# Attention and gated MLP in one kernel: the plain part in three chunks of 512 tokens in place of four of 384

## The chip, the cores and the metric

The kernel runs on one core of a Trainium2 chip. The metric is the device time of one execution in microseconds (us); 943.36 us is the median of three runs before the change (943.19 to 943.65). TensorE (PE in the profile; PEld is its weight load), VectorE (DVE), ScalarE (ACT), GpSimd (POOL) and SyncE (SP) each work through a queue of their own in order and wait on semaphores for one another. SP, ACT and POOL also issue the DMA transfers.

## The reference

Eight sequences of 576 positions, 8 heads of 64: attention with a causal window of 32 positions (heads 0 to 3) or of 32 positions four apart (heads 4 to 7), and then a gated MLP over all 4608 tokens, in float32:

```python
scores = scale * np.matmul(q, k.transpose(0, 1, 3, 2))      # (8, 8, 576, 576)
mask_plain = (rel >= 0) & (rel < window)                    # window = 32
mask_dil = (rel >= 0) & (rel < window * dilation) & (rel % dilation == 0)   # dilation = 4
attn = exp(scores - max) / (sum + 1e-9)                     # masked
x = np.matmul(attn, v)  ->  (4608, 512)
g = x @ w_gate                                              # 512 x 1536
y = (g * (1.0 / (1.0 + np.exp(-g))) * (x @ w_val)) @ w_out  # 1536 x 512
```

## The kernel before

**Precision.** Every MLP product is made of three matmuls in the type fp32r: a float32 operand is split into a high part (a cast) and a low part (operand minus high part), and high x high, high x low and low x high are added in PSUM.

**Two parts of the MLP.** The first T0 = 1536 tokens are the *plain part*: NPLAIN = 4 chunks of CH = 384 tokens. The other 3072 tokens go through a Strassen scheme (seven products in place of eight) in NCS = 3 chunks of two times 512 tokens, whose matmuls are those of L773.

**A step of the plain part** is one of the NF = 12 blocks of 128 hidden units of one chunk; there are NS = NPLAIN x 12 = 48 steps, `s` in the main loop. In a step, `gv_mm` (L459) makes 12 matmuls for the gate into `bank_g` and 12 for the value into `bank_v`, `act_tanh` (ACT, L468), `dve_u` (L473) and `dve_h` (L478) form h, `h_hi` (ACT, L483) and `h_lo` (POOL, L488) split it, and `out_mm` (L496) of the step before adds 12 matmuls to four output banks. So a step has 36 matmuls. `out_store` empties the output banks once in a chunk.

**Attention** is cut into *packs*: a pair of heads, a stretch of tokens, up to four *groups* of four blocks of 32 queries against 64 keys. The list of packs has 46 packs with 152 groups in all. A pack's work: `scores` (PE, L354, two heads x four blocks x groups matmuls of 64 columns; for the first packs the mask is added by two more, L348), `shift` (DVE, maximum L368 and subtraction L369), `exps` (ACT, L374), `turn_e` (PE, one transpose per group, L378), `keys` (ACT copy, L384), `results` (PE, L394), `norm` (DVE, L403 to L405), `turn_y` (PE, one transpose per group, L412), and a copy into the x of the MLP: high part by ACT (L429, or L444 in the head) and low part by DVE (L430, L448), or for Strassen chunks a plain copy (L438). Packs from the fifth on are placed by hand into *slots*, three to a step, in a table `visit`: at slot "A" of pack m the results of pack m-1 and the scores of m, at "B" the transposes.

**The head.** The four packs of chunk 0 (three groups each) run first, together with the first weight units, in an order for PE, DVE and ACT that is written out as a string: Q scores, S shift, X exps, T turn_e, K keys, A results, N norm, U turn_y, H and L the two parts of x, W0 to W4 the five stages of the next weight unit. What follows in the program is put in order by the framework's list scheduler, which may also set matmuls of the first step between those of the string; on the chip each engine then keeps that order.

**Weights.** The float64 weights come as 24 units of 768 KB (`w_load` on SP). Two units make the weights of one of the 12 hidden blocks; unit 2f has the gate and half of the value columns, unit 2f+1 the rest. Five stages turn them into high and low parts: E (ACT, L235), T (L253 on ACT or L256 on DVE, by `by_act`), B (DVE, L263 or L266), H (ACT cast, L274), L (POOL, L278). All 24 are made during the steps of chunk 0, by `w_upto`, two a step. Raw units lie in six buffers.

**Mixing.** During the later chunks the weights are combined for the Strassen part and written to DRAM in pieces: 9 x NP = 54 stages (`mix_stage`, DVE L650 to L663, ACT L660), called from the main loop by `mix_to` twice a step from step 12 on, `half * 54 // 62` of them by half step `half`, so the last at half step 62.

Of the kernel before, what the change touches and what calls it, by code (L numbers as in the profile page):

```python
# [11 lines left out]
F32R = mybir.dt.float32r  # L12
# [6 lines left out]
P = 128  # L19
D = 64  # L20
S = 576
DIL = 4
CH = 384
DM = 512
# [18 lines left out]

NPLAIN = 4
CS = 512
# [15 lines left out]
T0 = NPLAIN * CH  # L61
KINDS = "aoooFooboooo"
NM = len(KINDS)

# [71 lines left out]
def attention_moe(ctx, tc, qkb, vb, w, masks, ident, out):  # L136
# [3 lines left out]
    def pk(m):  # L140
        return PACKS[m]
# [5 lines left out]
    M_ATT = M_SMALL + 40  # L147
    M_X1 = M_ATT + QKB + 4 * NGM * (D + 1) + 3 * TP
    M_SPARE = M_X1 + 2 * NK * CH
    NSPARE = 1352  # L150
    M_H = M_SPARE + NSPARE
    M_RAW = M_H + 5 * CH
    M_X0 = M_RAW + 8 * WU
    M_W = M_X0 + 2 * NK * CH
    M_RING = M_W + NT * 4 * CS
    M_HQ = M_RING + NAT * PIECE
    assert M_HQ + 5 * NP * CS <= M_W + 2 * WB * NF
    M_LOW = M_RAW + PIECE
    M_OT = M_LOW + 2 * PIECE + CS
    assert M_OT + 4 * CH + 2 * CS <= M_X0  # L160
    origin = -(-nc.sbuf_base // 64) * 64
# [24 lines left out]
    consts = at(0, (NM * BK + P) // 2, BF16)  # L186
    mask_sb, ident16 = consts[:, :NM * BK], consts[:, NM * BK:]

# [5 lines left out]

    WARM = 24
    wt = [at(M_W + 2 * WU * u, 2 * WU, F32R) for u in range(NU)]

# [12 lines left out]
    loaded = 0  # L210
    raw_at = [M_RAW + 2 * WU * n for n in range(4)] + [M_LATE + 2 * WU * n for n in range(2)]
    raw_of = {}
    YW = 3 * UT + 8

    def w_load():
        nonlocal loaded
        u = loaded
        n = u % 6 if u < NU - NLAST else (u + 2) % 4
# [20 lines left out]
    def by_act(u):  # L239
        return u in (1, 2) or u > 3 and u % 2 == 1  # L240

# [3 lines left out]
    def w_shift(u):  # L245
        n = u - NU + NLAST
        y = at(M_LATE + 4 * WU + YW * (u % 3) if n < 0 else M_SPARE if n == 0 else raw_at[(u + 1) % 4], YW, I32)
        wst[u]["y"] = y[:, :3 * (UT + 1)].rearrange("p (a b) -> p a b", a=3)[:, :, :UT]
# [65 lines left out]
    early, later = {}, {}  # L314
    for k, n, fn, fb in (("qk", QKB, FQ, 4), ("v", 4 * NGM * (D + 1), 4 * FG * (D + 1), 3), ("e", TP, P * FG, 2),
                         ("y", TP, P * FG, 2), ("pt", TP, P * FG, 2)):
        later[k] = Ring(n, o)
        o += n
    o = M_ATT
    for k, fn, fb in (("qk", FQ, 4), ("v", 4 * FG * (D + 1), 3), ("e", P * FG, 2), ("y", P * FG, 2), ("pt", P * FG, 2)):  # L320
        step = -(-fn // 8) * 8
        early[k] = Ring(fn, *range(o, o + step * fb, step))
        o += step * fb
    assert o <= M_H
    for k, a in (("bm", M_SMALL), ("bz", M_SMALL + 16)):
# [84 lines left out]
    def turn_y(m, bank):  # L410
        for g in range(pk(m).ng):
# [3 lines left out]
    x32 = [[at(o, 2 * CS).rearrange("p (k c) -> p k c", k=2) for o in x]  # L415
           for x in ((M_OT + 4 * CH, M_X0), (M_SPARE, M_X0 + 2 * CS))]

    def x_views(m, bank, *x):
        if pk(m).ng * P == CH:
            return bank[:, :CH], *x  # L420
        n = len(pk(m).runs)
        return (bank[:, :P * pk(m).ng].rearrange("p (n t) -> p n t", n=n)[:, :, :CH // n],
                *(t.rearrange("p (n t) -> p n t", n=n) for t in x))

    def x_copies(m, bank):
        c = pk(m).chunk
        if c < NPLAIN:
            src, xh, xl = x_views(m, bank, *(t[c % 2][pk(m).pair] for t in (x_hi, x_lo)))
            nc.scalar.copy(out=xh, in_=src)  # L429
            nc.vector.tensor_tensor(out=xl, in0=src, in1=xh, op=ALU.subtract)  # L430
        else:
# [10 lines left out]
    def x_copy_hi(m, bank):  # L442
        src, xh, xl = x_views(m, bank, *(t[0][pk(m).pair] for t in (x_hi, x_lo)))
        nc.scalar.copy(out=xh, in_=src)  # L444

    def x_copy_lo(m, bank):
        src, xh, xl = x_views(m, bank, *(t[0][pk(m).pair] for t in (x_hi, x_lo)))
        nc.vector.tensor_tensor(out=xl, in0=src, in1=xh, op=ALU.subtract)  # L448
        st[m].clear()


# [11 lines left out]
    t_ring = Ring(CH, M_H, M_H + CH)  # L463
    hh_ring = Ring(CH, M_H + 2 * CH, M_H + 3 * CH)

# [20 lines left out]
    def h_lo(i):  # L486
        hl = at(M_H + 4 * CH, CH, F32R)
        nc.gpsimd.tensor_tensor(out=hl, in0=hst[i][0], in1=hst[i][1], op=ALU.subtract)  # L488
        hst[i][2] = hl
# [9 lines left out]
    def out_store(ci):  # L499
        for j in range(4):  # L500
            ot = at(M_OT + CH * j, CH)
            if j % 2 == 0:
# [13 lines left out]

    bank_x, bank_k, bank_r, *s_banks = [bank(ab, *x) for x in (("fx", 1), ("fk", 1), ("fr", 2), ("fs0", 2), ("fs1", 2))]


    load_qk(0, fa, nc.sync)  # L520
    nc.scalar.dma_start(out=consts, in_=masks)
    load_qk(1, fa, nc.scalar)
    load_v(0, fa, nc.sync)
    nc.sync.dma_start(out=idents, in_=ident.rearrange("n p c -> p n c"))
    nc.vector.memset(ones, 1.0)
# [4 lines left out]
    warm = ones.bitcast(BF16)  # L530
    for _ in range(WARM):
        nc.tensor.matmul(out=bank_x[:, :P], lhsT=warm, rhs=warm, start=True, stop=True)
    load_qk(2, fa, nc.sync)
    load_v(1, fa, nc.sync)
    w_load()
    load_qk(3, fa, nc.sync)
    load_v(2, fa, nc.sync)
    w_load()

    def more_in():  # L540
        load_v(3, fa, nc.sync)
        w_load()
        ready["w"] = True

# [6 lines left out]
        "U": lambda m: turn_y(m, x_bank[m]), "H": lambda m: x_copy_hi(m, x_bank[m]),  # L551
        "L": lambda m: x_copy_lo(m, x_bank[m]), "M": lambda m: more_in(), "W": lambda n: w_one(STAGES[n]),
# [26 lines left out]

    M1 = 4 * NPLAIN + 10  # L580
    for n in range(5):
        visits(4 + n, 5 + 13 * n // 2, 8 + 13 * n // 2)
    for n in range(4):
        visits(9 + n, 39 + 25 * n // 3, 43 + 25 * n // 3)
    for m in range(13, M1 + 1):
        a = SB - 75 + 49 * (m - 13) // 10
        visits(m, a, a + 3)
# [5 lines left out]
    def attend(now):  # L593
        what, m = visit.get(now, ("", 0))
        if what == "A":
# [6 lines left out]
            if m < NPK:  # L602
                shift(m, two, later, m < 8)
                exps(m)
                load_v(m, later, nc.scalar)
                if m + 1 < NPK:
# [23 lines left out]

    q_at = at(M_RAW, PIECE)
    l_at = at(M_LOW, 2 * PIECE, F32R).rearrange("p (n l c) -> p n l c", n=4, l=2)

# [80 lines left out]

    x1 = at(M_X0 + 4 * CS, 2 * CS).rearrange("p (k c) -> p k c", k=2)
    HS = 10
    own = [M_SPARE + 2 * CS, M_SPARE + 4 * CS, M_OT, M_X1 + 4 * CS]
    NOWN = len(own)
    assert own[1] + 2 * CS <= M_RAW
    kept = [[at(M_X1 + CS * (2 * k + r), CS) for r in range(2)] for k in range(2)]  # L720
    temps = [M_RAW + CS * n for n in range(7)] + [M_OT + 2 * CS]
    g_ring = Ring(CS, *temps[:3])
# [192 lines left out]
def layout(q, k, v, moe_w_gate, moe_w_val, moe_w_out):  # L915
# [17 lines left out]
    w = np.ascontiguousarray(w.reshape(NF, P, 2, WU).transpose(0, 2, 1, 3))  # L933
    masks = np.concatenate([block_masks(), np.eye(P)], axis=1).astype(ml_dtypes.bfloat16)
    order = np.arange(P).reshape(DIL, BQ).T.ravel()
# [21 lines left out]
```

## Time and profile before

| what | value |
| --- | --- |
| median of three runs | 943.36 us |
| the profiled execution: its time | 943.46 us |
| the profiled execution: its span | 941.7 us |
| PE, PEld, DVE, ACT, POOL busy | 99%, 86%, 67%, 42%, 26% of the span |
| first matmul of the plain part, its last run (L496) | starts at 19.8 us, holds the chain from 382.0 to 384.1 us |
| last run of matmuls | holds the chain from 921.4 to 938.0 us |

A profile's page lists the busy time of each engine, the span in 40 slices, the DMA queues, the chain of work that ended last, and the costliest groups of instructions. The chain in order of time gives for each piece its start and the time that it held the chain, in us; for a run of matmuls (x12) that is the time until the next piece takes over. In the timeline the two first numbers are start and length in us, and the brackets give the engine's idle time before the instruction and what ended it. A row of the groups ends in busy time in us and mean length of one in ns, then the idle time before them. A row of the stretches gives for each engine busy us and instructions, then the granted clock of TensorE, the share of the DMA engines and GB/s.

### The profile page before, as it was taken

The page shows a single profiled execution, that of the slowest core. Times are in us where ns is not written, and L with a number is a line of the kernel's source. Part 1 is how long each engine was busy: PE and PEld are TensorE (multiplying, and loading weights), DVE is VectorE, ACT ScalarE, POOL GpSimd, SP SyncE. Part 2 cuts the span into 40 slices and gives each one's busy share as a digit, 9 for nine tenths or more (in the row PEclk, how much of TensorE's full clock was granted, in tenths as well). Part 3 has the DMA queues.
Part 4 walks back from the last instruction along what each step waited for, and adds up shares of the span by engine and source line. Part 5 has one row for each costly group of instructions (what it writes and reads, how often), then busy time and mean ns, then how long its engine had stood idle before and what let it go on. Part 6 is the DMA issues. An engine that isn't in the chain of part 4 may idle for free.

```text
span 941.7 us, 21975 instructions
## 1 busy us (share of the span) xinstructions
PE 929.6 (99%) x9204; PEld 813.0 (86%) x9204; DVE 632.9 (67%) x1072; ACT 393.1 (42%) x687; POOL 249.4 (26%) x301
## 2 busy tenths in 40 slices
PE   7899999999999999999999999999999999999998
PEld 5799999999999999888888888888888888888886
DVE  4767566666677865666669965666689735656863
ACT  4885323233233333333344643343355523334451
POOL 0765421111111131123233121222223213343310
PEclk9999999999999999999999999999999999999999
DMA  9976156577757791676767768676766675656662
GB/s 370 337 283 200 36 203 214 177 238 238 242 183 243 248 323 43 219 237 213 236 215 236 245 219 260 222 240 199 255 202 197 210 257 186 198 186 195 198 207 107
DMA packets 75394, 205.26 MB, mean 218 GB/s; under 512 B 7584, under 2 KB 24096, under 8 KB 75296
## 3 DMA queue, kind: packets, MB, share of 16 engines
q0 software_dynamic: 27216, 99.10, 33.6%
q1 hardware_dynamic: 35696, 64.93, 19.4%
q10 hardware_dynamic: 12384, 39.83, 12.5%
q8 instruction: 72, 1.18, 0.5%
q14 instruction: 26, 0.21, 0.1%
HBM read 161.37 MB, written 42.47 MB: 216 GB/s over the span
## 4 chain that ended last, share of the span: by engine, by line
PE 96%; ACT 1%; DVE 1%; issue 1%; DMA 0%; DVEq 0%; ACTq 0%
PE bo L773 32%; PE bv L773 12%; PE bg L773 12%; PE bo L496 10%; PE bv L459 10%; PE bg L459 10%; PE two L394 3%; PE two L354 3%; PE two L378 2%; PE two L412 2%; DMA at_bfloat<-masks 0%; ACT at_float32r L274 0%; ACT at_int L235 0%; DVE at_int L266 0%; DVE at_int L263 0%
## 5 line engine op out<-in xcount | busy, mean ns | idle before, releaser
L773 PE MATMUL bo<-at_float32r 128*128 128x512 f32 x1296 | 308.5, 392 | 0.0
L773 PEld LDWEIGHTS bo<-at_float32r 128*128 128x128 f32 x1296 | 242.2, 188 | 51.9 <-ACT at_float L503 0.2
L701 POOL DMA_DIRECT2D at_float32r<-pieces x189 | 101.4, 537 | 381.0 <-PE bo L773 219.2
L736 DVE TENSOR_TENSOR at_float<-bo,at_float 128x512 f32<-128x512 f32 (+1 forms) x169 | 114.2, 684 | 106.0 <-ACT at_float L778 50.2
L736 DVE TENSOR_TENSOR at_float32r<-at_float,at_float32r 128x512 fp32r<-128x512 f32 (+1 forms) x147 | 115.1, 806 | 41.7 <-ACT at_float32r L763 28.7
L773 PE MATMUL bv<-at_float32r 128*128 128x512 f32 x486 | 130.0, 394 | 0.0
L773 PE MATMUL bg<-at_float32r 128*128 128x512 f32 x486 | 129.8, 393 | 0.0
L488 POOL TENSOR_TENSOR at_float32r<-at_float,at_float32r 128x384 fp32r<-128x384 f32 x48 | 54.8, 1142 | 220.2 <-PE bo L496 175.7
L459 PE MATMUL bg<-at_float32r,at_float32r 128*128 128x384 f32 x576 | 110.9, 339 | 2.1 <-DVE at_float L473 1.3
L459 PE MATMUL bv<-at_float32r,at_float32r 128*128 128x384 f32 x576 | 110.1, 338 | 0.0
L496 PE MATMUL bo<-at_float32r,at_float32r 128*128 128x384 f32 x576 | 110.1, 338 | 0.0
L773 PEld LDWEIGHTS bv<-at_float32r 128*128 128x128 f32 x486 | 90.2, 188 | 19.5
L773 PEld LDWEIGHTS bg<-at_float32r 128*128 128x128 f32 x486 | 90.3, 188 | 19.2
L763 ACT CAST at_float32r<-at_float 128x512 fp32r<-128x512 f32 x126 | 77.3, 622 | 69.7 <-PE bo L773 23.8
L459 PEld LDWEIGHTS bg<-at_float32r,at_float32r 128*128 128x128 f32 x576 | 99.9, 188 | 3.8 <-POOL at_float32r L278 1.1
L496 PEld LDWEIGHTS bo<-at_float32r,at_float32r 128*128 128x128 f32 x576 | 100.2, 188 | 0.9
L459 PEld LDWEIGHTS bv<-at_float32r,at_float32r 128*128 128x128 f32 x576 | 99.7, 188 | 0.8
L799 ACT ACTIVATE at_float<-at_float 128x512 f32<-128x512 f32 x72 | 45.6, 633 | 81.0 <-DVE at_float L736 80.8
L473 DVE SCALAR_TENSOR_TENSOR at_float<-at_float,bg 128x384 f32<-128x384 f32 x48 | 26.6, 554 | 76.8 <-ACT at_float L468 76.8
L778 ACT COPY at_float<-bg 128x512 f32<-128x512 f32 x63 | 37.0, 587 | 95.5 <-PE bg L773 95.3
L801 DVE SCALAR_TENSOR_TENSOR at_float<-at_float,at_float 128x512 f32<-128x512 f32 x72 | 49.5, 687 | 10.6 <-ACT at_float L799 10.5
L278 POOL TENSOR_TENSOR at_float32r<-at_int,at_float32r 128x768 fp32r<-128x768 f32 x24 | 45.8, 1917 | 40.7 <-ACT at_float32r L274 40.5
(79 smaller groups left out, 904.5 us busy)
## 6 DMA issues: line engine op xcount, KB each, us to landing
at_float32r<-pieces POOLq DMA_DIRECT2D x189, 512.0 KB, 3.9
pieces<-at_float32r SPq DMA_DIRECT2D x126, 256.0 KB, 4.6
at_int<-w SPq DMA_DIRECT2D x24, 768.0 KB, 6.2
at_float<-vb ACTq DMA_DIRECT2D x28, 390.0 KB, 5.0
at_float<-vb ACTq DMA_DIRECT2D x14, 520.0 KB, 5.2
at_float<-qkb ACTq DMA_DIRECT2D x14, 448.0 KB, 5.4
out<-at_float SPq DMA_DIRECT2D x23, 256.0 KB, 4.0
at_float<-qkb ACTq DMA_DIRECT2D x10, 544.0 KB, 6.0
```

What stands on the lines that cost most here:

```text
L278: nc.gpsimd.tensor_tensor(out=lo, in0=wst.pop(u).bitcast(F32), in1=hi, op=ALU.subtract)
L354: nc.tensor.matmul(out=two[BQ * j:BQ * j + BQ, h, a + BK * g:a + BK * g + BK], lhsT=t[r, q:q + BQ], rhs=t[r, k:k + BK], start=not masked, ...
L459: nc.tensor.matmul(out=bank[:, :CH], lhsT=wcol(f, o, low), rhs=x[ORDER[j]], start=n == 0, stop=n == len(ops) - 1)
L488: nc.gpsimd.tensor_tensor(out=hl, in0=hst[i][0], in1=hst[i][1], op=ALU.subtract)
L496: nc.tensor.matmul(out=bank_o[j][:, :CH], lhsT=wcol(f, 2 * DM + P * j, low), rhs=x, start=f == 0 and low == 0 and x is hh, stop=f == NF - ...
L701: nc.gpsimd.dma_start(out=taken[asked], in_=pieces[asked % NPIECE])
L736: engine.tensor_tensor(out=out, in0=a, in1=b, op=op)
L763: nc.scalar.copy(out=o[:, 0], in_=src)
L773: nc.tensor.matmul(out=bank, lhsT=w, rhs=x, start=first and n == 0 and t in FRESH, stop=last and n == len(ops) - 1, skip_group_check=True)
L778: nc.scalar.copy(out=kept[KEPT[t]][r], in_=banks[0][r][:, :CS])
L799: nc.scalar.activation(out=f, in_=g, func=AF.Tanh, scale=0.5)
L801: nc.vector.scalar_tensor_tensor(out=f, in0=f, scalar=1.0, in1=g, op0=ALU.add, op1=ALU.mult)
```

## The change

`CH` becomes 512 and `NPLAIN` 3, so the plain part has 36 steps of matmuls with 512 columns. The packs of the plain part are cut anew: four packs of 512 tokens (four groups each) for chunk 0, six for each of the chunks 1 and 2; the list again has 46 packs and 152 groups, and from the 17th on it is the same. The table `visit` follows: packs 4 to 10 every 13/3 slots in chunk 0, packs 11 to 26 every four slots from slot 37 on. Mixing is called at `half * 54 // 41`, so it ends at half step 41 after chunk 0 (step 32 of 36).

SBUF is shared out anew: the buffers of the four early packs move into the place of weight units 8 to 15, the transposed keys (`pt`) share the buffer of the scores (`e`), raw weights have five buffers in place of six, high parts of h one in place of two, and the Strassen part's buffers move. `h_hi` is written behind `out_mm` of the step before, which reads the one buffer.

The head: another string, other loads first (masks in two parts, the second late), 9 warm-up matmuls of 512 columns in place of 24 of 128, four more of them between the first packs (`Y2` twice), and other units whose stage T is done by ACT.

```diff
-CH = 384
+CH = 512
-NPLAIN = 4
+NPLAIN = 3
...
-    out = [Pack(c, p, CH * c, CH * c + CH) for c in range(NPLAIN) for p in ORDER]
+    out = [Pack(0, p, 0, CH) for p in ORDER]
+    for c, cut in ((1, 704), (2, 1280)):
+        a, b = CH * c, CH * c + CH
+        out += [Pack(c, p, lo, hi) for p, lo, hi in ((0, a, b), (2, a, cut), (1, a, b), (2, cut, b), (3, a, cut),
+                                                      (3, cut, b))]
...
-    WARM = 24
+    WARM = 9
...
-    raw_at = [M_RAW + 2 * WU * n for n in range(4)] + [M_LATE + 2 * WU * n for n in range(2)]
+    raw_at = [M_RAW + 2 * WU * n for n in range(3)] + [M_LATE + 2 * WU * n for n in range(2)]
...
-        return u in (1, 2) or u > 3 and u % 2 == 1
+        return u == 0 or u % 2 == 1
...
+    o = M_W + 16 * WU
+    for k, n, many in (("qk", FQ, 4), ("v", 4 * FG * (D + 1), 4), ("e", P * FG, 4), ("y", P * FG, 2)):
...
+    for x in early, later:
+        x["pt"] = Ring(x["e"].n, *x["e"].starts)
...
-    hh_ring = Ring(CH, M_H + 2 * CH, M_H + 3 * CH)
+    hh_ring = Ring(CH, M_H + 2 * CH)
...
-    for _ in range(WARM):
-        nc.tensor.matmul(out=bank_x[:, :P], lhsT=warm, rhs=warm, start=True, stop=True)
+    def idle(n):
+        for _ in range(n):
+            nc.tensor.matmul(out=bank_x.rearrange("p (a b) -> p a b", a=4), lhsT=warm,
+                             rhs=warm.unsqueeze(1).broadcast_to([P, 4, P]), start=True, stop=True)
+    idle(WARM)
...
-        for what in ("Q0 Q1 S0 X0 T0 S1 K0 X1 A0 M0 W0 Q2 N0 T1 K1 S2 X2 Q3 W1 W0 S3 X3 A1 U0 N1 W2 T2 K2 H0 L0 W3 W4 "
-                     "T3 A2 K3 W1 U1 N2 A3 H1 L1 W0 W2 U2 N3 W3 H2 U3 L2 W4 H3 L3 W1 W0 W2 W1 W2 W3 W0 W0").split():
+        for what in ("Q0 S0 Q1 Y2 S1 X0 T0 Y2 K0 X1 Q2 T1 S2 A0 K1 W0 N0 W1 U0 X2 W2 A1 H0 L0 W3 Q3 N1 W4 W1 T2 S3 U1 "
+                     "K2 W0 A2 X3 N2 H1 T3 W2 K3 U2 A3 H2 L1 W0 N3 W3 L2 W0 W4 U3 W1 H3 L3 W0 W2 W1 W1 W3 W1 W4 W2 W0").split():
...
-    load_qk(4, later, nc.sync)
+    with tc.issue_after(last["w"].ins):
+        load_qk(4, later, nc.sync)
...
+    for m in range(4, 11):
+        a = 5 + 13 * (m - 4) // 3
+        visits(m, a, a + 3)
+    for m in range(11, M1 + 1):
+        a = NB + 1 + 4 * (m - 11)
         visits(m, a, a + 3)
...
-        while mixed < half * 9 * NP // 62:
+        while mixed < half * 9 * NP // 41:
...
         dve_h(s)
-        h_hi(s)
         with tc.issue_after(last["h"].ins):
             w_upto(T=W + 6, B=W + 6)
         if s > 0:
             out_mm(s - 1)
+        h_hi(s)
         h_lo(s)
```

More of the change, by code (lines that the diff above doesn't have):

```diff
@@ L217, in w_load @@
         u = loaded
-        n = u % 6 if u < NU - NLAST else (u + 2) % 4
+        n = u % 5 if u < NU - NLAST else u % NLAST % 3
         if u >= NU or raw_of.get(n, -1) >= done["B"]:
@@ L415, in attention_moe @@
     x32 = [[at(o, 2 * CS).rearrange("p (k c) -> p k c", k=2) for o in x]
[L416 to L423, printed above, removed]
+           for x in ((M_XE, M_X1), (M_XE + 2 * CS, M_X1 + 2 * CS))]
     def x_copies(m, bank):
@@ L427, in x_copies @@
         if c < NPLAIN:
-            src, xh, xl = x_views(m, bank, *(t[c % 2][pk(m).pair] for t in (x_hi, x_lo)))
-            nc.scalar.copy(out=xh, in_=src)
-            nc.vector.tensor_tensor(out=xl, in0=src, in1=xh, op=ALU.subtract)
+            xh, xl = [t[c % 2][pk(m).pair] for t in (x_hi, x_lo)]
+            for col, first, n in pk(m).runs:
+                first -= CH * c
+                src, h, l = bank[:, col:col + n], xh[:, first:first + n], xl[:, first:first + n]
+                nc.scalar.copy(out=h, in_=src)
+                nc.vector.tensor_tensor(out=l, in0=src, in1=h, op=ALU.subtract)
         else:
@@ L530, in attention_moe @@
     warm = ones.bitcast(BF16)
-    for _ in range(WARM):
-        nc.tensor.matmul(out=bank_x[:, :P], lhsT=warm, rhs=warm, start=True, stop=True)
+    def idle(n):
[3 more added lines that the diff above has]
+    idle(WARM)
     load_qk(2, fa, nc.sync)
+    w_load()
     load_v(1, fa, nc.sync)
+    load_qk(3, fa, nc.sync)
     w_load()
-    load_qk(3, fa, nc.sync)
     load_v(2, fa, nc.sync)
+    load_v(3, fa, nc.sync)
     w_load()
[L540 to L543, printed above, removed]
+    w_load()
+    nc.sync.dma_start(out=consts[:, near:], in_=masks[:, near:])
+    while w_load():
+        pass
+    ready["w"] = True
     x_bank = [bank_x, bank_x, s_banks[0][:, 0], s_banks[1][:, 0]]
@@ L577, in visits @@
         visit[a], visit[b] = ("A", m), ("B", m)
[L580 to L586, printed above, removed]
+    M1 = len([x for x in PACKS if x.chunk < NPLAIN]) + 10
+    for m in range(4, 11):
[3 more added lines that the diff above has]
+        a = NB + 1 + 4 * (m - 11)
         visits(m, a, a + 3)
@@ L604, in attend @@
                 exps(m)
-                load_v(m, later, nc.scalar)
+                if m > 4:
+                    load_v(m, later, nc.scalar)
+                else:
+                    with tc.issue_after(last["w"].ins):
+                        load_v(m, later, nc.sync)
                 if m + 1 < NPK:
```

71 lines of the change are left out of this document (31 added, 40 removed).

## The prediction

> **What bounds the kernel now.** I read the page first, then the chain in order of time, then the timeline of the first 50 us.
>
> ```profile
> span 941.7 us, 21975 instructions
> PE 929.6 (99%) x9204; PEld 813.0 (86%) x9204; DVE 632.9 (67%) x1072; ACT 393.1 (42%) x687; POOL 249.4 (26%) x301
> ...
> PE 96%; ACT 1%; DVE 1%; issue 1%; DMA 0%; DVEq 0%; ACTq 0%
> ```
>
> TensorE holds 96% of the chain that ends last. So the change pays only if PE's queue gets shorter or if PE waits less, and PE waits only in the head. Its queue, first in the plain part, where some steps have no attention between their matmuls, then in the Strassen part:
>
> ```profile
> 166.98 0.33 PE two L412 x3
> 167.30 0.33 PE two L378 x3
> 167.63 2.10 PE bg L459 x12
> 169.74 2.08 PE bv L459 x12
> 171.81 2.10 PE bo L496 x12
> ...
> 178.10 0.59 PE two L394 x41
> 178.69 0.54 PE two L354 x32
> 179.23 2.28 PE bo L496 x12
> ```
>
> ```profile
> 828.40 1.36 PE bg L773 x6
> 829.76 1.36 PE bv L773 x6
> 831.12 2.72 PE bo L773 x12
> ```
>
> Twelve matmuls of 384 columns hold the chain for 2.09 us (mean of 2.10, 2.08 and 2.10), 174.3 ns each; twelve of 512 for 2.72 us, 226.7 ns each. The 128 further columns cost 52.4 ns, 0.41 ns a column; at that price 384 columns are 157 ns, and 17 ns of each matmul are paid whatever its width. That is what wider chunks save. The rows also give the price of attention: 0.33 + 0.33 + 0.59 + 0.54 = 1.79 us for a pack of three groups, 0.6 us a group, and some 0.2 us beside (2.28 after a visit, 2.09 else).
>
> The head, from the timeline:
>
> ```profile
> 1.00 2.74 PE L532 MATMUL fx<-at_float 128*128 128x128 bf16 x24 [1.00 <-DVE at_float L527]
> ...
> 8.12 0.90 PE L378 MATMUL fk<-at_float,at_float 128*128 128x128 f32 x3 [0.28 <-ACT at_float L374]
> ...
> 19.47 0.55 PE L412 MATMUL fx<-at_float,at_float 128*128 128x128 f32 x3
> ...
> 24.55 0.56 DVE L448 TENSOR_TENSOR at_float32r<-fs,at_float32r 128x384 fp32r<-128x384 f32 x1 [0.21 <-ACT at_float32r L444]
> ...
> 27.80 1.63 PE L459 MATMUL bg<-at_float32r,at_float32r 128*128 128x384 f32 x8 [0.61 <-DVE at_float L473]
> ...
> 36.08 1.16 PE L459 MATMUL bg<-at_float32r,at_float32r 128*128 128x384 f32 x5 [0.74 <-DVE at_float L473]
> ```
>
> The last low part of x is ready at 25.11 us (24.55 + 0.56). Step 1 starts at 27.80, step 2 at 36.08: 8.3 us for 36 matmuls that need 6.3, and the idle times in the brackets lead to DVE. By 36.08 PE has done 60 plain matmuls (gate and value of two steps, the output of one) and the attention of 12 groups. One more wait of size follows:
>
> ```profile
> PE two L378 <- ACT at_float L374: 0.8, 1, 0.8
> ```
>
> From there on PE is full. The three transposes that took 0.90 us at 8.12 take 0.55 at 19.47.
>
> **The change part by part.**
>
> *Wider matmuls.* Before: 48 steps x 36 = 1728 matmuls. After: 36 x 36 = 1296. In runs of twelve, 144 x 2.09 = 301.0 us become 108 x 2.72 = 293.8: 7.2 us less. It is all on PE's queue.
>
> [...]
>
> *Attention.* By the code 46 packs and 152 groups before and after, so as many visits; PE's sum is the same. But four packs of four groups are now in the head, 16 groups in place of 12: 4 x 0.6 = 2.4 us of PE's later work move into a time when PE waits anyway.
>
> *The head.* I reckon to T', the time when 60 plain matmuls are done (36.08 before). A pack of four groups has longer work on ACT and DVE:
>
> ```profile
> L374 ACT ACTIVATE at_float<-at_float 128x384 f32<-128x384 f32 x32 | 16.8, 524 | 29.6 <-DVE at_float L369 29.5
> ...
> L405 DVE TENSOR_TENSOR at_float<-two,at_float 128x384 f32<-128x384 f32 x28 | 15.6, 557 | 0.9
> ...
> L405 DVE TENSOR_TENSOR at_float<-two,at_float 128x512 f32<-128x512 f32 x14 | 9.7, 690 | 0.5
> ...
> L374 ACT ACTIVATE at_float<-at_float 128x512 f32<-128x512 f32 x14 | 8.8, 632 | 16.0 <-DVE at_float L369 16.0
> ```
>
> ACT has three passes over a pack (exp, keys, high part), each longer by 632 - 524 = 0.11 us: 0.33 a pack, 1.3 for four. DVE has four (maximum, subtraction, product, low part), each by 0.13: 0.53, 2.1 for four. The chain through the four packs goes over both in turns, so the last low part comes later by 1.3 us (only ACT's counts) to 3.4 (both). Against that stands PE's pace. Three transposes lost 0.35 us each time while PE was slow, and four such passes lie ahead of 18 us; with a longer and thicker warm-up (9 matmuls of 512 columns, and four more between packs) that can be 0 to 1.4 us sooner. So the last low part ends between 25.0 (25.11 + 1.3 - 1.4) and 28.5 us; middle 26.75. About half of step 0's 24 gate and value matmuls must wait for it: 12 x 0.227 = 2.7 us. Then come 36 more without a stall: 8.2 us. T' = 26.75 + 2.7 + 8.2 = 37.65, ends 35.9 and 39.4.
>
> [...]
>
> Why no stall in step 1: before, units 2 and 3 came late because a step of 6.3 us asks for two units; now it has 8.2 us. And the transfers? In the string's time the queues are full:
>
> ```profile
> 5.00:10.00 5.00, 4.04 (x135) 2.55 (x136) 2.23 (x4) 1.43 (x3) 0.00 (x0) 1.00 1.06 417
> ```
>
> At 417 GB/s what stands ahead of and in unit 0 is 3.33 MB after (qk of packs 0 to 2, v of pack 0, near masks, the identities, the unit) and 3.27 MB before; for unit 1 5.2 MB against 4.9, 0.8 us later, and it is wanted only when pack 2's x is made. Those are covered. If not, each us of delay is a us of T'.
>
> After T' PE still has 1236 matmuls x 0.2267 = 280.2 us (before 1668 x 0.1743 = 290.7): 10.5 less. The 2.4 us of attention and the 0.8 us wait fall away too. So the end of the plain part moves by 37.65 - 36.08 - 10.5 - 2.4 - 0.8 = -12.1 us. (As two terms: 7.2 from width, 4.9 from the head.)
>
> *At nothing, with their cover.* `h_hi` behind `out_mm`: with one buffer it waits for the first eight of those matmuls, 8 x 0.227 = 1.8 us behind the value's end, when `dve_h` is just done; the next `out_mm` comes 36 matmuls, 8.2 us, after that end. Behind it on ACT stand weight stages, a pack's exps and the next tanh, which is not due before 2 x 2.72 = 5.4 us. If that cover were gone, each late us would come 36 times. `pt` in `e`'s place: the next subtraction already stands behind the results that read it. Five raw buffers: two units per 9.5 us instead of 7.5. The first later pack's loads move behind the weights on SP; its scores are due only in step 1. Split copies of x: one more small instruction on ACT and DVE, off the chain. The last `out_store` has copies of 512 in place of 384 columns between two users of a bank: 0.1 us on PE.
>
> *DVE in the middle* is the one cover that gets thinner:
>
> ```profile
> 115.00:352.00 237.00, 237.00 (x3115) 230.29 (x3114) 163.92 (x325) 78.05 (x149) 39.73 (x39) 1.00 0.68 227
> ```
>
> In this stretch, nearly all mixing and 14 packs, DVE was busy 163.9 us and PE never idle. After, about the same DVE work falls in 20.5 steps: 20.5 x 8.2 + 14 packs x 2.0 = 196 us of PE, 84%. I take no stall, bounds 0 and 4 us. A gain is excluded, since PE was never idle there.
>
> Sum: against the profiled execution's 943.46 us (its span 941.7 and 1.8 around it; the median is 0.1 lower) -12.1 + 0.1. On the median: 943.36 - 12.0 = **931.4 us**. Its own range: T' from 35.9 to 39.4, and a stall of 1.5, is 929.6 to 934.7.
>
> **The rivals.**
> 1. *Width alone.* The head gives back what it gains: T' at 42.5, say because PE stays slow and the longer packs queue on ACT. Then 943.4 - 7.2 = 936.2, with small stalls of the middle 935 to 940. For: ACT and DVE are the chain there and get more work. Against: step 1's stall had its cause in too short a step. Chance 0.22.
> 2. [...] Chance 0.03.
> 3. *Slower: DVE becomes the bound* in chunks 1 and 2, in steps 12 to 32, where mixing is pressed together. It decides when DVE needs more than PE's 196 us, and passes the whole gain at 208, 27% above the row's 163.9. At 33% it needs 218, 22 us past PE, and the time is 953. For: packs every four slots and mixing by 41. Against: 84%. Chance 0.05.
> 4. *The change doesn't get its order*: the scheduler, not the string, decides what PE does after the string, and a matmul put too early blocks those behind it. The head then costs up to the gain: 943, within 0.2% of before. Chance 0.04.
>
> The forecast keeps 0.66.
>
> **How the numbers follow.** Two runs of this kernel can be told apart from about 0.2%, 1.9 us. Slower by that: rival 3 and a bad end of 4, 0.06. Same: the rest of 4 and an end of 1, 0.04. Faster: 0.90. The range from 928.0 (T' a little below its end, no stall) to 938.0 takes in the forecast, most of rival 1 and rival 2.
>
> **What would show it.** Right: runs of twelve at 2.72 us on L459 and L496, the first matmul of step 2 at 36 to 39 us, the last matmul of the plain part about 12 us sooner, PE full from there, the Strassen part as long as before. Wrong: runs of 2.9 or more (rival 2 in the other part: a wait on bank or weight), a step 2 after 42 us (rival 1), idle PE before L459 with DVE as releaser between 100 and 300 us (rival 3), slow transposes after 10 us for the clock's part.

## The result, and the profile after

The changed kernel takes 949.77 us (median of five runs, 949.37 to 953.4), the kernel before, beside it, 943.65 us (943.19 to 944.87). The ratio is 1.0077 with a 95% interval of 1.0054 to 1.0100: slower by 0.8%, where 931.4 us was forecast, and outside the range of 928.0 to 938.0. The profiled execution of the changed kernel took 952.9 us, 3.1 above its median; the traces below are compared with the 943.46 us of the one before.

The page of the changed kernel: span, busy times, and shares of the chain that ended last.

```profile
span 951.1 us, 21018 instructions
PE 926.4 (97%) x8761; PEld 754.6 (79%) x8761; DVE 637.7 (67%) x1049; ACT 391.0 (41%) x664; POOL 242.4 (25%) x289
PE 87%; DMA 5%; DVE 4%; ACT 2%; issue 2%; SPq 0%; ACTq 0%; DVEq 0%
```

PE is busy for 3.2 us less, which goes the way that wider matmuls should, and yet the span is 9.4 us longer. The chain tells more: PE fell from 96% to 87%, and DMA, which had 0%, has 5%. Something waits for transfers. PE's own list of waits (total us, times, longest) shows where:

```profile
PE two L395 <- DVE at_float32r L427: 9.2, 4, 6.3
PE fr L395 <- issue: 5.1, 3, 2.4
PE two L379 <- ACT at_float L375: 1.9, 1, 1.9
...
PE two L355 <- DMA at_float<-qkb: 0.9, 1, 0.9
```

The first is results of a pack that wait for the bank which the x of an earlier pack is still being copied out of; no line of the kernel before is of that kind, and its largest are small:

```profile
PE bg L459 <- DVE at_float L473: 1.3, 2, 0.7
PE fs L354 <- issue: 1.2, 1, 1.2
```

DVE is named, but DVE is not short of time. In the stretch that the prediction looked at (engines in the order PE, PEld, DVE, ACT, POOL) it worked 166.7 us, against 163.9 before:

```profile
115.00:352.00 237.00, 235.49 (x2650) 192.11 (x2648) 166.73 (x309) 79.06 (x139) 42.33 (x34) 1.00 0.65 220
```

The timeline around the longest of these waits shows who made DVE late:

```profile
100.98 3.01 PE L453 MATMUL bv<-at_float32r,at_float32r 128*128 128x512 f32 x12
103.56 0.90 ACT L236 ACTIVATE at_int<-at_int 128x768 f32<-128x768 f32 x1 [4.27 <-DMA at_int<-w]
104.36 0.60 ACT L477 CAST at_float32r<-at_float 128x512 fp32r<-128x512 f32 x1
...
106.39 0.57 ACT L462 ACTIVATE at_float<-bg 128x512 f32<-128x512 f32 x1
...
107.66 0.45 ACT L385 COPY at_float<-two 128x384 f32<-128x384 f32 x1
...
108.02 0.57 ACT L426 CAST at_float32r<-two 128x512 fp32r<-128x512 f32 x1
108.65 0.96 DVE L266 SCALAR_TENSOR_TENSOR at_int<-at_int,at_int 128x768 int32<-128x768 int32 x1
109.53 0.68 DVE L427 TENSOR_TENSOR at_float32r<-two,at_float32r 128x512 fp32r<-128x512 f32 x1
...
110.27 0.96 PE L395 MATMUL two<-at_float,at_float 64*32 64x65 f32 x47 [6.27 <-DVE at_float32r L427]
...
111.61 4.45 PE L490 MATMUL bo<-at_float32r,at_float32r 128*128 128x512 f32 x12
```

Read the brackets backwards. PE waits 6.27 us for DVE's low part of x. That waits for ACT's high part (L426), and then for a weight stage of DVE (L266) that ran first. The high part stands in ACT's queue behind the keys (L385), the tanh (L462), the high part of h (L477) and further weight stages. All of these stand behind one E stage (L236) for which ACT sat idle for 4.27 us, until a raw weight unit landed. It is the 22nd unit, and its block of hidden units has its first matmul at 134.5 us, three steps later; the stage only stood first in an in-order queue. ACT's list of waits has this for the whole run, the changed kernel first, the kernel before second:

```profile
ACT at_int L236 <- DMA at_int<-w: 17.8, 9, 4.3
```

```profile
ACT at_int L235 <- DMA at_int<-w: 6.0, 4, 2.8
```

The last line of the timeline is a second price. Twelve matmuls of 512 columns take 4.45 us after the wait, though the chain has runs of twelve that take 2.7:

```profile
48.21 2.72 PE bv L453 x12
50.93 2.73 PE bo L490 x12
```

After the waits of 1.83 us (at 70) and 6.27 us, eight and seven matmuls start some 427 ns apart instead of 227: 15 x 0.2 = 3.0 us. The granted clock of those stretches (the third number from the end) is half:

```profile
73.75:77.16 3.41, 3.41 (x9) 2.63 (x10) 2.88 (x6) 1.03 (x2) 1.65 (x2) 0.50 0.79 242
...
107.88:114.71 6.83, 4.44 (x87) 3.66 (x88) 6.69 (x10) 2.38 (x4) 2.52 (x3) 0.50 0.28 81
```

The 1.9 us in front of the transposes (L379) are another matter. They stand at 352.7 us, when all weights are made: exps behind a DVE that had worked all but without a pause since 345.6, during the mixing.

The other part of the loss is in the head. The chain there (start, us held), and then the end of x on DVE:

```profile
11.57 1.40 issue
...
16.72 2.42 issue
...
24.02 1.31 issue
...
28.27 0.79 ACT at_int L236
29.06 0.72 ACT at_float32r L274
29.78 0.83 ACT at_int L236
...
44.41 0.86 PE two L355 x53
```

```profile
31.14 0.69 DVE L443 TENSOR_TENSOR at_float32r<-fs,at_float32r 128x512 fp32r<-128x512 f32 x1
```

Three times PE waited for nothing that the profile shows, 5.1 us in all (before, 1.2 us once, at 11.87); then weight stages of ACT stand between the last high parts of x. The last low part of x ends at 31.83 us, and T' (60 plain matmuls done) is 45.2 us.

The table sums the distances from the start of one PE matmul to the start of the next in the traces, up to the last one (us, differences to before in brackets; attention between the Strassen matmuls is in the rest). Its last column is the experiment that follows first.

| stretch | before | forecast | after | e_behind_tanh |
| --- | --- | --- | --- | --- |
| up to T' | 36.1 | 37.65 (+1.6) | 45.2 (+9.1) | 45.0 (+8.9) |
| from T': plain matmuls and the waits behind them | 298.0 | (-11.3) | 301.1 (+3.1) | 289.4 (-8.6) |
| from T': attention and the waits behind it | 44.2 | (-2.4) | 43.2 (-1.0) | 41.8 (-2.4) |
| the rest, nearly all Strassen | 559.4 | (+0.1) | 557.4 (-2.0) | 557.4 (-2.0) |
| sum | 937.6 | -12.0 | 946.9 (+9.3) | 933.6 (-4.1) |

### The profile page after: what moved, and what is told of

It is laid out like the page before. It is cut to its first block, busy times and chain, and to the rows that moved or that the text cites. A ratio compares the mean times of both kernels' runs of the same rounds, so it can differ in the third digit from the quotient of the medians.

```text
span 951.1 us, 21018 instructions
## 1 busy us (share of the span) xinstructions
PE 926.4 (97%) x8761; PEld 754.6 (79%) x8761; DVE 637.7 (67%) x1049; ACT 391.0 (41%) x664; POOL 242.4 (25%) x289
## 4 chain that ended last, share of the span: by engine, by line
PE 87%; DMA 5%; DVE 4%; ACT 2%; issue 2%; SPq 0%; ACTq 0%; DVEq 0%
PE bo L778 31%; PE bv L778 12%; PE bg L778 12%; PE bo L490 8%; PE bg L453 8%; PE bv L453 8%; DMA at_int<-w 3%; PE two L395 3%; PE two L355 2%; PE two L379 1%; PE two L413 1%; DMA at_float<-qkb 1%; DMA pieces<-at_float32r 1%; DVE at_int L263 1%; DMA at_bfloat<-masks 0%
## 5 line engine op out<-in xcount | busy, mean ns | idle before, releaser
L490 PE MATMUL bo<-at_float32r,at_float32r 128*128 128x512 f32 x432 | 109.3, 403 | 0.0
L453 PE MATMUL bg<-at_float32r,at_float32r 128*128 128x512 f32 x432 | 107.3, 395 | 0.6 <-DVE at_float L467 0.6
L453 PE MATMUL bv<-at_float32r,at_float32r 128*128 128x512 f32 x432 | 106.5, 394 | 0.0
L482 POOL TENSOR_TENSOR at_float32r<-at_float,at_float32r 128x512 fp32r<-128x512 f32 x36 | 47.9, 1332 | 208.4 <-PE bo L490 123.2
L490 PEld LDWEIGHTS bo<-at_float32r,at_float32r 128*128 128x128 f32 x432 | 81.9, 193 | 17.8 <-issue 0.2
L453 PEld LDWEIGHTS bg<-at_float32r,at_float32r 128*128 128x128 f32 x432 | 79.7, 188 | 18.6 <-DVE at_float L467 1.3
L453 PEld LDWEIGHTS bv<-at_float32r,at_float32r 128*128 128x128 f32 x432 | 80.0, 188 | 16.9
L467 DVE SCALAR_TENSOR_TENSOR at_float<-at_float,bg 128x512 f32<-128x512 f32 x36 | 24.7, 686 | 74.3 <-ACT at_float L462 74.3
L278 POOL TENSOR_TENSOR at_float32r<-at_int,at_float32r 128x768 fp32r<-128x768 f32 x24 | 45.2, 1891 | 73.4 <-ACT at_float32r L274 69.7
```

What stands on the lines that cost most here:

```text
L278: nc.gpsimd.tensor_tensor(out=lo, in0=wst.pop(u).bitcast(F32), in1=hi, op=ALU.subtract)
L453: nc.tensor.matmul(out=bank[:, :CH], lhsT=wcol(f, o, low), rhs=x[ORDER[j]], start=n == 0, stop=n == len(ops) - 1)
L490: nc.tensor.matmul(out=bank_o[j][:, :CH], lhsT=wcol(f, 2 * DM + P * j, low), rhs=x, start=f == 0 and low == 0 and x is hh, stop=f == NF - ...
```

## The experiments

Theory A: E stages, put ahead of tanh in ACT's order, wait for raw weights and hold up what stands behind them; one raw buffer fewer makes the loads late. Theory C: PE's three pauses in the head are its own instructions arriving late behind full DMA queues. Rivals: B, the packs' slots leave too little time between copy and results (so the wait is the table's); D, the written order of the head; and that E's place is worth the same in any kernel.

### A sixth raw buffer (raw6)

```diff
-    raw_at = [M_RAW + 2 * WU * n for n in range(3)] + [M_LATE + 2 * WU * n for n in range(2)]
+    raw_at = [M_RAW + 2 * WU * n for n in range(3)] + [M_LATE + 2 * WU * n for n in range(-1, 2)]
...
-        n = u % 5 if u < NU - NLAST else u % NLAST % 3
+        n = u % 6 if u < NU - NLAST else u % NLAST % 3
...
-    while w_load():
-        pass
+    w_load()
```

> The changed kernel with a sixth buffer for raw weight units (in the home of unit 19, which is free until stage H of unit 19). Theory A (stage E of a weight unit stands at the head of ACT's in-order queue and waits for a load that could only start when stage B of the unit five earlier freed its buffer; tanh, keys and x copies stand behind it and PE waits for them): ACT's wait on the load of w falls from 17.8 us to under 9, PE's wait for the low part of x (L427) from 9.2 us to under 3, and the time from 949.8 to 938 to 943. Rival B (the table of visits leaves only 1 to 1.3 slots, 2.7 to 3.6 us, between a pack's x copies and the next results, which write the same bank, and any delay there stalls PE): PE's wait stays over 6 us and the time over 946.

948.3 us, ratio 1.0046 (1.0031 to 1.0061). ACT's wait fell from 17.8 to 12.9 us and PE's behind L427 from 9.2 to 5.8: less than theory A expected, and the time stayed where rival B had it. The 1.5 us less than the changed kernel are not clear of noise, as the two intervals overlap. So the missing buffer is at most a part of the cause: with six buffers ACT still waits twice as long as in the kernel before.

### Transposes one slot earlier (visit2)

```diff
-        visits(m, a, a + 3)
+        visits(m, a, a + 2)
```

(at both places of the plain part)

> The changed kernel with slot B of each plain-part visit two slots behind slot A in place of three, so that x copies have 2 to 2.3 slots (5.4 to 6.3 us) before the next results write the same bank. Theory A alone (ACT waits for raw weights): ACT's wait on the load of w stays near 17.8 us; the stalls on PE shrink by the one slot each, from 9.2 us to 4 to 6; time 944 to 948. Rival B (too tight a table): PE's wait on L427 falls below 2 us and the time to 938 to 943.

953.08 us, ratio 1.0102 (1.0071 to 1.0134). PE's waits:

```profile
PE two L379 <- ACT at_float L375: 5.8, 7, 2.1
...
PE two L413 <- DVE at_float L370: 4.5, 2, 3.1
```

The wait at L395 went, as rival B had it, but not the time with it: as much came back in front of the transposes, behind exps (ACT) and shift (DVE), and the time lies above what either side expected. ACT still waited 14.9 us for raw weights. Rival B falls: the table can choose where PE meets the late work, not that it is late.

### E behind tanh (e_behind_tanh)

```diff
-        nc.scalar.activation(out=t, in_=bank_g[:, :CH], func=AF.Tanh, scale=0.5)
+        last["t"] = nc.scalar.activation(out=t, in_=bank_g[:, :CH], func=AF.Tanh, scale=0.5)
...
-        w_upto(L=W + 3, H=W + 4, E=W + 6)
+        w_upto(L=W + 3, H=W + 4)
         gv_mm(ci, f, 0)
         act_tanh(s)
+        with tc.issue_after(last["t"].ins):
+            w_upto(E=W + 7)
...
-        w_upto(L=W + 4, H=W + 5, E=W + 7)
+        w_upto(L=W + 4, H=W + 5)
```

> The changed kernel with both E stages of a step tied behind that step's tanh in ACT's queue, still five raw buffers. Theory A in its form about the order (E is placed ahead of need, so ACT stands idle on a load that nobody wants yet): ACT's wait on the load of w falls below 6 us, PE's wait on L427 below 3 us, time 938 to 943. If the loads themselves come too late for the weights (a supply limit), PE waits for weights in L453 instead and the time stays over 946. Rival B expects little change, 947 to 950.

939.47 us, ratio 0.9954 (0.9939 to 0.9969): 10.3 us less than the changed kernel, and 0.5% faster than the kernel before. Its page and ACT's waits:

```profile
span 937.8 us, 21014 instructions
...
PE 923.8 (99%) x8761; PEld 752.7 (80%) x8761; DVE 639.0 (68%) x1049; ACT 391.3 (42%) x664; POOL 243.8 (26%) x289
```

```profile
ACT at_int L253 <- DMA at_int<-w: 7.0, 5, 2.8
ACT at_int L236 <- DMA at_int<-w: 0.4, 1, 0.4
```

ACT still waits for weights, 7.4 us in all, in another place, nearly all of it at stage T (L253). Of the 9.2 us behind L427 there are 0.5 left, in two waits, and no plain matmul after T' starts 427 ns behind another. T' stayed at 45.0, so all of this gain lies behind T'. Theory A holds, and the stage's place is the larger part of it. The wait in front of the transposes in the mixing is still there, at 339.4 us, with 0.8 us.

### The same in the kernel before (before_e_behind_tanh)

The same edit in the kernel before.

> The kernel before with both E stages of a step tied behind that step's tanh. If the order of E cost time only where the change made ACT less busy (in the kernel before, E mostly runs 2 to 9 us after its unit has landed and PE has no wait over 0.8 us after 37 us), the time stays within 1.5 us of 943.7. If E's order cost the kernel before as much, it falls by 4 us or more.

946.28 us, ratio 1.0021 (1.0012 to 1.0030): 2.4 us slower, a little more than the 1.5 us that were expected at most. E's old place cost the kernel before nothing that the tie gives back, and the tie (E only after tanh) brought a wait of its own near 45 us, where 0.8 us had stood:

```profile
PE two L378 <- ACT at_float L374: 2.7, 1, 2.7
```

The profiled execution was one of the shorter (944.71 us), so this wait need not be all of the loss. The loss of the changed kernel is not one that the kernel before had as well; and the edit is a cure for this order, not a rule.

### Six raw buffers and E behind tanh (raw6_e)

> The changed kernel with E tied behind tanh (939.5 us) and six raw weight buffers. If what was lost in the middle is gone with E's place, the sixth buffer adds little: 938 to 940. If loads are still late for the stages behind them (ACT still waits 7.0 us for raw weights at L253), ACT's wait falls under 4 us and the time to 936 to 938.

939.81 us, ratio 0.9959 (0.9946 to 0.9972), as without the sixth buffer. ACT still waits 8.3 us for raw weights at L253, and the time doesn't show it: with little that PE needs behind the late load, its lateness was next to free.

### The order of before in the head (old_string)

On top of e_behind_tanh, the string of the kernel before.

> The changed kernel with E tied behind tanh (939.5 us) and with the head's written order of the kernel before (no idle matmuls between the packs). Theory C (while the DMA queues are full a block of 256 records of PE's queue comes no sooner than about 6.2 us after the one before it, and the head of larger packs has a block more to fetch): PE's gaps stay at records 449, 705 and 961 or are hidden by slower work there, and the 61st plain matmul starts within 2 us of 45.0. Rival D (the new written order is what makes the head late, since it puts stage E of unit 1 behind the keys of pack 2, at 22.7 us): the 61st plain matmul starts 3 us or more sooner, and the time falls to 935 to 937.

940.63 us, ratio 0.9962 (0.9946 to 0.9977), T' 44.0. The chain in its head:

```profile
16.68 1.76 issue
...
23.01 1.59 issue
```

Counted in the trace (weight loads, matmuls and the waits for semaphores in PE's queue), PE's pauses stand behind its instructions 449, 705 and 961 in this order as in the changed one: every 256th, whatever the instruction is. Behind 449 it is now a score (L355), in the changed order a result (L395). Rival D falls. In the kernel before the same 449 has the pause of 1.2 us, inside scores; 705 and 961 show no pause over 0.3.

The fetch of PE's instructions is itself in the traces. The changed kernel's page has it among the DMA queues (packets, MB, share of the engines):

```profile
q8 instruction: 69, 1.13, 0.5%
```

That is one packet of 16,384 bytes for every 256 or so of PE's 17,522 weight loads and matmuls. By the trace's record of packets the first three in the head end at 11.47, 17.85 and 24.06 us, and PE goes on at 12.97, 19.14 and 25.33. In 14 of the 15 traces PE has such pauses behind 449, 705 or 961, 30 in all, and each ends 1.3 to 1.6 us after a packet (the fifteenth, few_in_flight, has none). So PE waits for its instructions; what delays them is what the next runs ask.

### Loads held back, three ways (late_loads, w2_later, few_in_flight)

late_loads asks for units 1 to 4 from ACT's queue from 16 us on; w2_later (on e_behind_tanh) does so with units 2 to 4 at some 22 us. (In both, SP asks for unit 5 at 15.8 us, ahead of them, since its buffer is the first to be free; so the queues were emptied less than the expectations say.) few_in_flight (on e_behind_tanh) leaves the order and makes SP wait, by rewriting 16 words of v buffers, until an earlier transfer has landed.

```diff
+    def landed_v(m):
+        nc.sync.dma_start(out=st[m]["v"][:1, 0, :16], in_=vb[m, :1, :16])
...
     load_qk(2, fa, nc.sync)
+    landed_v(0)
     w_load()
...
```

> The changed kernel with raw weight units 1 to 4 asked for later, from ACT's queue behind W3 (about 17 us) and later, so that the queues run empty of weights between about 14 and 17 us. Theory C (PE's gaps in the head at its records 449, 705 and 961, 256 apart, are waits for its next block of instructions, whose fetch stands among the transfers): the gaps of 2.4 and 1.3 us at records 705 and 961 shrink to under 0.5 us, the gap at 449 (1.4 us) stays, and the 61st plain matmul starts 2 to 4 us sooner than 45.2 us; the time falls by 2 to 4 us unless the weights then come late. Rival (the gaps are waits of the results for something of the kernel): they stay, and the time is the same or up to 3 us longer.

> The changed kernel with E tied behind tanh (939.5 us), and with weight units 2 and later asked for only behind the keys of pack 2 (about 22 us). Theory C: the queues run empty of weights from about 18 us, so the gap at record 961 falls from 1.6 us to under 0.5, that at 705 (18.6 us) by half at most; the 61st plain matmul starts 0 to 2 us sooner if the weights are still in time, and later if they are not (unit 2 is wanted at 28 us). Rival (gaps not from the transfers): the gap at 961 stays.

> The changed kernel with E tied behind tanh (939.5 us), and with SyncE held back in the head until an earlier v has landed (it writes 16 of that v's words again, with the same values), so that about four transfers are under way in place of eight. Theory C in the form that the fetch stands behind the transfers that are queued: the time from record 449 to 705 falls from 6.2 us to under 5, the gaps at 705 and 961 from 2.7 and 1.6 us to under 1.5 and 1, the 61st plain matmul starts 2 to 4 us sooner than 45.0, the time falls by 2 to 4 us. If only the load of the DMA engines counts and not the number queued, the gaps stay within 0.5 us and the time is the same or a little longer.

late_loads: 960.14 us (1.0158 to 1.0192 times before), the pause at 961 gone, at 705 still 2.1 us, weights late, T' 53.5. w2_later: 947.36 us (1.0013 to 1.0039), 961 gone, 705 still 2.5 us, T' 49.5, with a wait of 3.9 us ahead of step 1, whose weights came late. few_in_flight: 943.29 us (0.9988 to 1.0013), all three pauses gone, T' 47.4. There the DMA engines stayed busy (the share is the number ahead of the last):

```profile
10.00:15.00 5.00, 2.98 (x138) 2.23 (x136) 3.02 (x6) 3.64 (x7) 0.00 (x0) 1.00 0.97 323
```

But PE waited 4.3 us for the rewritten words, just ahead of 705, and 3.2 us ahead of step 1, whose weights came late; behind that first wait a pause at 705 could not show. The packets of instructions tell more. In the changed kernel they start 3.5, 3.8 and 3.8 us after PE has begun the block of 256 before. In w2_later and thin (below), where PE enters the third of these blocks at the same 19.14 us, but with little or nothing left in line, the packet starts after 1.1 us. In few_in_flight it is 1.7, 3.5 and 2.2 us at shares of 0.93 to 1.00 in the four stretches of 5 us from 5 to 25 us, so full engines alone don't make the delay; fewer transfers in line made two of three shorter. The pauses hang on the loads, and each of the three edits pays more for it than it gains.

### Lighter tokens (tokens, tokens_raw6)

The same as few_in_flight, with other words that are rewritten: spare columns in the q and k of packs 1 and 3, and 16 words of pack 0's v; tokens_raw6 adds the sixth buffer.

> The changed kernel with E tied behind tanh (939.5 us), and with fewer transfers under way in the head: three small rewrites of words that have landed (spare columns of the q and k of packs 1 and 3, and 16 words of pack 0's v) hold SyncE back, and no results wait for the first and third of them. Theory C (PE's next block of 256 records is fetched behind whatever is queued): the gaps at records 449 and 705 fall from 0.8 to 1.4 and 2.7 us to under 0.5 and 1, the 61st plain matmul starts at 41 to 43.5 us in place of 45.0, and the time is 936 to 938. Rival (the head's lateness is not the fetch but the larger packs' own work and the weights): T' stays at 44.5 or later and the time at 939 or more.

> Both of the two other kernels' edits. By theory C and a useful sixth buffer the gains add: 934 to 937. If the head's gain is only moved (weights made later by the held-back loads), it is no better than the better of the two.

940.6 us (ratio 0.9945 to 0.9974) and 939.46 us (0.9948 to 0.9975): no different from e_behind_tanh, and what the rivals expected. The pause at 705 went in the first and fell to 0.56 us in the second, the one at 961 stayed (2.2 and 2.1 us), and PE waited 1.6 to 1.7 us for a token; T' 44.4 and 43.4.

### Fewer bytes in the head (thin, before_thin)

On e_behind_tanh, and on the kernel before as a control:

```diff
-        last["w"] = nc.sync.dma_start(out=t, in_=w[u // 2, u % 2].bitcast(I32))
+        k = 192 if 0 < u < 6 else 2 * WU
+        last["w"] = nc.sync.dma_start(out=t[:, :k], in_=w[u // 2, u % 2].bitcast(I32)[:, :k])
...
```

> This kernel is e_behind_tanh with one edit: weight units 1 to 5 load an eighth of their words (192 of 1536 a partition; the rest of each raw slot is filled with a constant by POOL first), so that the DMA queues are free of weights early, and the weight stages keep their places and their lengths. The weights of those units are not the reference's, and the output isn't either. Theory (the pauses of PE at records 705 and 961 are its instructions coming late behind full DMA queues): both pauses fall under 0.7 us, T' (the time by which PE has done its first 60 plain matmuls) goes from 45.0 to 39 to 41 us, and the time from 939.5 to 934 to 936 us. Rival (the pauses come from the work of the head itself, and weights and queues have no part in them): the pauses stay at 2 to 2.7 and 1.3 to 1.6 us, T' stays within 1 us of 45.0, and the time within 1 us of 939.5. Second rival (the queues make the pauses, but PE's slow clock in the head has another source): pauses gone, T' 42 to 43.5, time 937 to 938.5.

> The kernel before with the same edit (units 1 to 5 load an eighth of their words, so the output isn't the reference's). It shows what the thinner loads are worth by themselves. Theory: the kernel before has one pause in its head, 1.2 us at record 449 amid the scores, and its queues delay little else: T' 36.1 goes to 34.5 to 36.1, the time from 943.7 to 942 to 943.7. Rival (thin loads free any head by the same amount, so that the new head has no trouble of its own): the time falls by as much as it does in thin.

thin: 943.32 us (ratio 0.9983 to 1.0009); before_thin: 945.03 us (1.0002 to 1.0019). The time of neither run is one that was expected. The queues of thin were free from about 17 us:

```profile
15.00:20.00 5.00, 3.08 (x81) 1.92 (x89) 2.02 (x5) 2.11 (x3) 1.72 (x1) 0.50 0.56 192
20.00:25.00 5.00, 4.92 (x142) 4.14 (x142) 2.77 (x6) 2.45 (x5) 0.00 (x0) 0.57 0.03 7
```

The pause at 961 is gone, as theory C has it; the one at 705 (at 17.25 us, 1.9 us) is not: its packet started at 16.61 us, when the queues were still full. But T' is 44.98, as good as unchanged (44.97), for this came in its place:

```profile
PE bg L454 <- DVE at_float L468: 2.7, 1, 2.7
```

L468 waits for the tanh. The gate's last matmuls were done by 32 us; ACT came to the tanh at 34.35, behind six weight stages of 0.8 to 0.95 us that follow the last high part of x:

```profile
29.11 0.57 ACT L441 CAST at_float32r<-fs 128x512 fp32r<-128x512 f32 x1
29.57 0.91 ACT L237 ACTIVATE at_int<-at_int 128x768 f32<-128x768 f32 x1
...
33.63 0.86 ACT L275 CAST at_float32r<-at_int 128x768 fp32r<-128x768 f32 x1
34.35 0.64 ACT L463 ACTIVATE at_float<-bg 128x512 f32<-128x512 f32 x1
```

A pause less in PE's stream leaves T' where ACT's weight stages put it. Behind T' the trace of thin is 2.7 us longer than that of e_behind_tanh, and one wait of 2.5 us for the low part of x is nearly all of it. ACT came to the tanh there 2.5 us later than in e_behind_tanh (68.95 against 66.47 us), and to the keys and the high part behind it; what made the tanh late is not shown. It is the same wait as the changed kernel's of 1.83 us, but no slow clock follows it:

```profile
72.83 0.46 PE L396 MATMUL two<-at_float,at_float 64*32 64x65 f32 x32 [2.52 <-DVE at_float32r L428]
...
74.33 2.58 PE L491 MATMUL bo<-at_float32r,at_float32r 128*128 128x512 f32 x10
```

## Why the prediction was wrong, point by point

- **Wider matmuls, 7.2 us: right in kind, somewhat too large.** Runs of twelve take 2.72 us, as forecast. From start to start inside the runs the matmuls stand 173.8 and 227.5 ns apart (the run rows gave 174.3 and 226.7), which makes 1728 x 0.1738 - 1296 x 0.2275 = 5.5 us. Rival 2's smaller gain from the width (chance 0.03, and a part of the range) is a term that no run shows; the runs showed these 5.5 us in its place.
- **Attention, 2.4 us of it moved ahead of T': right** (2.4 in e_behind_tanh).
- **"At nothing, with their cover": this failed, and is the largest term.** The prediction put at nothing what stands on ACT behind `out_mm`, "weight stages, a pack's exps and the next tanh", and counted the five raw buffers as a matter of rate. It gave the weight stages no wait of their own. But an E stage waits for a load, and it stood in ACT's queue ahead of tanh, keys and the copies of x, which PE needs within a step. 9.2 us of waits behind L427 and 3.0 us of slow matmuls after two of them are in the changed trace after T'; the edit of E's place alone gave back 10.3 us. The evidence was in the profile of before, 6.0 us of ACT waiting for raw weights, and the prediction took no note of that row.
- **The head, T' = 37.65: wrong by 7.6 us, the other large term.** x was to end at 26.75 and ended at 31.83. The sum counted ACT's and DVE's passes over the packs. It had no term for PE's pauses (5.1 us on the chain against 1.2 before), nor for ACT's three weight stages between the last two high parts of x (2.3 us on the chain). From the end of x to T' it took 13.4 us instead of 10.9; a wait of 0.9 us for the q and k of the first later pack, which the prediction called covered, and one of 0.6 us for DVE ahead of step 1 are in that.
- **The clock's gain in the head ("0 to 1.4 us sooner"): there at first, then lost.** That a longer warm-up makes PE faster sooner was the author's estimate, and no run shows it by itself: the two heads differ in more than the warm-up. The kernel before has the full clock on record from 18.15 us. The granted clock of the changed kernel was full from 5.48 us, half from 15.72 to 22.55 us, and full from then on up to T'. The first four transposes took 0.66 us, four at 21 us took 1.11. The fall came 1.0 us ahead of the pause of 2.42 us, so it is not that pause which made it.
- **DVE in the middle, no stall: nearly right.** DVE had 166.7 us of work there, and PE had one wait of size, 1.85 us at 352.7 (0.8 in e_behind_tanh), for work behind a full DVE; the bounds were 0 and 4 us. Rival 3 is wrong as a mechanism for the loss, although its sign (idle PE with DVE as the releaser) is close to what the trace shows and its 953 us is near the measured time. A releaser is the last link of a chain, not its cause.
- **Rival 1 (T' at 42.5, and 935 to 940) was nearest for the head:** 45.0 and 939.5 us are what e_behind_tanh gave, though PE's pauses are not in it.
- **Not forecast:** the Strassen part is 2.0 us shorter in both kernels with the change; no run here says why.

**What stays open.** Why loads came late 12.9 us even with six buffers, against 6.0 before. How much of T' the pauses are worth: each run that removed one also made something else late, or met ACT's weight stages next. That the packets of instructions start late because of loads ahead of them is shown by the runs with little in line (1.1 us after PE began the block in w2_later and thin, 3.8 in the changed kernel); whether the number of transfers or their bytes decide it is not.

## What to carry to other kernels

Cost a moved or re-buffered stage not only by its length but by what it waits for, and list what stands behind it on its in-order engine: a stage that is two steps early for its user and waits for a load is safer behind the work that is due, where the load's lateness (7.4 us of ACT's waiting in e_behind_tanh) cost next to nothing here. Measure that too: the same tie cost the kernel before 2.4 us. Follow a wait from the named releaser back to the first engine that was itself idle; the engine named here had 30% to spare in the middle of the kernel. And look at waits of engines off the chain before a change makes them longer: 6 us of harmless waiting on ACT were the warning.

## What the runs showed of the hardware

- PE paused 0.6 to 2.9 us behind its 449th, 705th and 961st instruction while the DMA queues were full (in the changed kernel at shares of 1.02 to 1.04 from 5 to 25 us), in two written orders, and each pause ended 1.3 to 1.6 us after a packet of 16,384 bytes in the queue of instructions; in the changed kernel the blocks began 6.2 us apart (12.97, 19.14 and 25.33 us).
- After idle times of 1.83 and 6.27 us the matmuls of 512 columns ran at 427 ns for some 3 us, and after 2.52 us in thin, and 1.85 us at 350.9 in the changed kernel, at the full clock. The length of the idle time alone doesn't decide it. In the changed kernel the stretches of one granted clock between two recorded changes last 10.24, 6.83, 51.20, 3.41, 30.72, 6.83 and 836.26 us: 3, 2, 15, 1, 9, 2 and 245 times the shortest, 3.413 us. What makes the clock fall the traces don't show.
